# Reordering the stages of the first pass in a fused gated-attention and feed-forward kernel, moving weight rounding, state products, gates and the last sums

## Chip, cores and metric

One core of one Trainium2 chip. The metric is the device time of one execution in microseconds (us), median over runs. The kernel before takes 637.3 us (636.75 to 637.35, three runs).

Engines are named as in the profile: PE is TensorE (matrix products), PEld its weight loads, DVE is VectorE, ACT is ScalarE, POOL is GpSimd, SP is the engine that issues most transfers.

## The reference

Two parts, the first feeding the second. A gated linear attention keeps one 48x48 state for each of 8 heads and each batch; its rows become x of a feed-forward layer with 3072 tokens.

```python
f = 1.0 / (1.0 + np.exp(-f_logit))                    # the gate
for t in range(S):                                    # S = 768, B = 4, H = 8, D = 48
    state = f[:, :, t, :, None] * state + np.einsum('bhd,bhe->bhde', k[:, :, t], v[:, :, t])
    y[:, :, t] = np.einsum('bhd,bhde->bhe', q[:, :, t], state)
x = y.transpose(0, 2, 1, 3).reshape(B * S, H * D)     # 3072 x 384
h = x @ w_in                                          # 384 x 2048
sp = np.maximum(h, 0.0) + np.log1p(np.exp(-np.abs(h)))
return (h * erf(sp)) @ w_out                          # 2048 x 384
```

## The kernel before

The attention runs on chunks of 128 tokens, the feed-forward layer on blocks of two chunks. Chunks are numbered from 0, so the fourth chunk is chunk 3; the recorded texts also say "the sixth chunk" where they mean chunk 6, the first chunk of the fourth block. Each chunk passes four stages: `stage_d` (decays: a product of the gate's logarithms with a triangle, two exps on ScalarE, two multiplies on VectorE), `stage_t` (eight transposes, copied to `qT` and `kT`), `stage_s` (scores, their masking `A` on VectorE, then the state product `dS` and the sums `Sn` and `Mbd`) and `stage_y` (the chunk's output, copied to `xT`).

```python
def prepare(blk, j0, j1):                             # the gate of a block: log(1 + exp(-f))
    nc.vector.tensor_scalar(out=lt, in0=lt, scalar1=LOGIT_MIN, scalar2=None, op0=ALU.max)
    use_exp_ln()                                      # loads a function table, where another one is in
    nc.scalar.activation(out=lt, in_=lt, func=AF.Exp, scale=-1.0)
    nc.scalar.activation(out=lt, in_=lt, func=AF.Ln, bias=1.0)

def stage_s(g):
    sc = ...                                          # scores: 8 products
    A = ...; nc.vector.tensor_tensor(out=A, in0=sc, in1=tri, op=ALU.mult)
    if c == NCH - 1: return
    dS = ps_at.tile(..., tag="at")                    # a PSUM buffer that the next transposes need
    ...                                               # state products, 8
    for r in range(2):
        nc.vector.tensor_tensor(out=Sn[rows(r)], in0=dS[rows(r)], in1=old[...], op=ALU.add)
        nc.vector.tensor_tensor(out=new[...], in0=Sn[rows(r)], in1=total, op=ALU.mult)   # Mbd
    # total is Tall: the chunk's last row of decays, brought to other partitions by a transfer
# [cut]
```

Between the stages TensorE runs the feed-forward products. One such product is a "slot", and a schedule says at which slot which stage, which gate and which step of weight rounding (six on VectorE for each piece of 128x768, one on ScalarE) is issued:

```python
for it in range(n_blocks):
    gen, n = slots(it)
    if it == 0:
        todo = [(stage_d, 3), (stage_t, 3), (stage_d, 4), (stage_s, 3), (stage_t, 4), (stage_y, 3),
                (stage_d, 5), (stage_s, 4), (stage_t, 5), (stage_y, 4)] + stages(2)[4:]
        at = [3, 9, 12, 15, 20, 23, 36, 44, 60, 74, 78, 82, 86, 92]
    # [cut: later passes spread their stages evenly]
    if it + 3 < n_blocks:
        prepare_at = at[todo.index((stage_d, (it + 3) * CPB))] - 10     # the gate, 10 slots ahead
    for s, _ in enumerate(gen):
        due += 1 if it == 0 and s < 48 else 0.5       # rounding steps due at this slot
        # [cut: rounding, loads, stages that are due]
        if it == 0 and s == 5:
            prepare(2, 0, CPB)                        # the third block's gate
        if it + 3 < n_blocks and s == prepare_at:
            prepare(it + 3, 0, CPB)
```

The output product `project` ends with three sums on VectorE (`plus`) and the store. The kernel is scheduled by hand: the order in which this code issues instructions is the order in which each engine is given them, and that order is nearly all that the change alters.

## Time and profile before

| | before |
|---|---|
| median, range (3 runs) | 637.3 us, 636.75 to 637.35 |
| span of the profiled run | 635.8 us |
| TensorE busy | 610.8 us (96%) |
| VectorE, ScalarE busy | 428.5 us (67%), 354.2 us (56%) |
| mean granted clock | 0.992 |

TensorE is near its limit over the whole, so only its idle 25 us and the stretches of low clock can be had. The prediction below shows the lines by stretch and by wait. Two more places of the kernel before matter for what came out. The first is the gate that chunk 6 waits for in pass 0. These are timeline lines (start, duration, engine, line, operation, output<-input, in brackets the engine's idle time before it and what ended it), first ScalarE, then VectorE, then TensorE:

```profile
83.53 1.28 ACT L322 ACT_TABLE_LOAD   x1
89.43 0.84 ACT L339 ACTIVATE lt<-lt 128x768 f32<-128x768 f32 x1 [4.62 <-DVE lt L335]
...
88.84 0.55 DVE L335 TENSOR_SCALAR lt<-lt 128x768 f32<-128x768 f32 x1
...
91.20 0.91 PE L358 MATMUL ps_d<-lt,tri 128*128 128x384 f32 x2 [1.47 <-ACT lt L340]
```

The reader is to see that the gate's first step (L335) reaches VectorE only at 88.84, behind a queue of rounding and of the activation's multiply; ScalarE stands idle 4.62 us for it, and TensorE 1.47 us. The second place is in the steady passes, in the view of waits of TensorE's weight loads (us in total, times, longest):

```profile
PEld hps L513 <- DVE scratch L649: 1.0, 3, 0.4
```

Three waits of up to 0.4 us: nothing in a busy table, yet each is time of the bound engine.

### The profile page before, as it was taken

How to read it: one execution, taken by the hardware profiler on the slowest of the kernel's cores; microseconds unless marked ns; L12 is line 12 of the kernel's file. 1: busy time of each engine (PE TensorE's matmuls, PEld its weight loads, DVE VectorE, ACT ScalarE, POOL GpSimd, SP SyncE). 2: the span in 40 equal slices, each digit the busy share in tenths (PEclk: the TensorE clock that was granted, in tenths of full speed). 3: DMA queues.
4: the chain of work that ended last, by engine and by line, in shares of the span. 5: the costliest groups of instructions: out<-in, count | busy, mean ns of one | idle time of the engine just before them, and what ended most of it. 6: DMA issues, size and time to landing. Idle time of an engine off the chain costs nothing.

```text
span 635.8 us, 11231 instructions
## 1 busy us (share of the span) xinstructions
PE 610.8 (96%) x4727; PEld 536.7 (84%) x4727; DVE 428.5 (67%) x651; ACT 354.2 (56%) x421; POOL 25.7 (4%) x24
## 2 busy tenths in 40 slices
PE   8979899999998999999999999999999999999995
PEld 6857778788667889889889989988978989989995
DVE  4799999635899576586485584495585764756741
ACT  5354456657763675756664856666566446656200
POOL 0000000000392000000000000000000000000000
PEclk9999999999999999999999999999999999999998
DMA  9998802311211131031041041031000000000000
GB/s 198 244 278 230 258 13 51 73 26 28 51 31 32 28 75 26 14 88 26 14 89 25 14 89 25 13 76 32 19 26 1 2 26 1 10 17 1 26 26 29
DMA packets 120633, 37.02 MB, mean 58 GB/s; under 512 B 112384, under 2 KB 115456, under 8 KB 120576
## 3 DMA queue, kind: packets, MB, share of 16 engines
q1 hardware_dynamic: 118496, 35.84, 24.2%
q8 instruction: 39, 0.64, 0.4%
q10 hardware_dynamic: 2080, 0.39, 0.4%
q14 instruction: 18, 0.15, 0.1%
HBM read 31.46 MB, written 4.72 MB: 57 GB/s over the span
## 4 chain that ended last, share of the span: by engine, by line
PE 72%; DVE 15%; ACT 7%; issue 3%; DMA 2%; SPq 0%; POOL 0%; DVEq 0%; ACTq 0%; POOLq 0%
PE hps L513 30%; PE ops L641 28%; PE y L146 5%; PE sc L403 3%; PE ps_t L385 2%; PE ps_d L358 2%; ACT x L155 2%; DVE e L160 1%; DVE A L417 1%; DVE scratch L541 1%; DMA Hg<-in_moe_w_in_dram 1%; DVE w_in_sb L296 1%; DVE Hg L305 1%; PE dS L431 1%; DVE Hg L487 1%
## 5 line engine op out<-in xcount | busy, mean ns | idle before, releaser
L513 PE MATMUL hps<-xT,w_in_sb 128*128 128x256 f32 x1152 | 263.9, 384 | 1.0 <-ACT xT L460 0.6
L513 PEld LDWEIGHTS hps<-xT,w_in_sb 128*128 128x128 f32 x1152 | 216.5, 191 | 35.7 <-issue 2.6
L160 DVE SCALAR_TENSOR_TENSOR e<-x,e 128x1024 f32<-128x1024 f32 x96 | 120.0, 1250 | 23.6 <-ACT x L155 23.5
L155 ACT ACTIVATE x<-Hg,serf_bias 128x1024 f32<-128x1024 f32 x88 | 97.7, 1142 | 0.1
L641 PE MATMUL ops<-wT,Hg 128*128 128x192 f32 x352 | 86.8, 328 | 0.0
L152 ACT ACTIVATE e<-Hg 128x1024 f32<-128x1024 f32 x44 | 46.5, 1058 | 70.9 <-DVE Hg L487 70.4
L641 PE MATMUL ops<-wT,scratch 128*128 128x192 f32 x320 | 75.1, 326 | 0.8 <-DVE scratch L541 0.8
L641 PE MATMUL ops<-w_out_sb,Hg 128*128 128x192 f32 x352 | 74.3, 328 | 0.0
L487 DVE TENSOR_TENSOR Hg<-Hg,e 128x1024 f32<-128x1024 f32 x44 | 54.2, 1231 | 28.7 <-ACT e L485 28.6
L520 ACT COPY Hg<-hps 128x1024 f32<-128x1024 f32 x44 | 44.4, 1009 | 50.2 <-PE hps L513 49.8
L649 DVE TENSOR_TENSOR scratch<-scratch,ops 128x384 f32<-128x384 f32 (+1 forms) x44 | 21.1, 501 | 65.3 <-ACT scratch L657 56.2
L641 PEld LDWEIGHTS ops<-wT,Hg 128*128 128x128 f32 x352 | 61.7, 190 | 2.2 <-issue 0.2
L641 PEld LDWEIGHTS ops<-w_out_sb,Hg 128*128 128x128 f32 x352 | 60.0, 190 | 3.7 <-issue 1.2
L641 PEld LDWEIGHTS ops<-wT,scratch 128*128 128x128 f32 x320 | 55.8, 190 | 1.1 <-POOL wT L541 1.1
L485 ACT ACTIVATE e<-e 128x1024 f32<-128x1024 f32 x48 | 50.5, 1052 | 6.2 <-DVE e L160 6.2
L371 DVE TENSOR_TENSOR qd<-qn,dp 128x384 f32<-128x384 f32 x24 | 13.3, 556 | 52.9 <-ACT dp L361 52.9
L417 DVE TENSOR_TENSOR A<-sc,tri 128x1024 f32<-128x1024 f32 x24 | 29.3, 1219 | 14.8 <-PE sc L403 14.6
L641 PE MATMUL ops<-w_out_sb,scratch 128*128 128x192 f32 x160 | 39.1, 326 | 0.0
L460 ACT COPY xT<-y 128x384 f32<-128x384 f32 x24 | 11.5, 479 | 45.7 <-PE y L146 45.7
L146 PE MATMUL y<-A,vt 128*32 128x128 f32 x768 | 35.2, 277 | 1.3 <-ACT qT L391 1.2
L146 PEld LDWEIGHTS y<-A,vt 128*32 128x32 f32 x768 | 27.3, 109 | 8.2 <-issue 3.8
L403 PEld LDWEIGHTS sc<-qT,kT 48*128 48x128 f32 x384 | 24.1, 193 | 7.6 <-issue 6.3
(108 smaller groups left out, 658.8 us busy)
## 6 DMA issues: line engine op xcount, KB each, us to landing
lt<-in_f_logit_dram SPq DMA_DIRECT2D x24, 192.0 KB, 3.5
qn<-in_q_dram SPq DMA_DIRECT2D x24, 192.0 KB, 3.7
out_dram<-scratch SPq DMA_DIRECT2D x12, 384.0 KB, 3.2
kn<-in_k_dram SPq DMA_DIRECT2D x23, 192.0 KB, 3.7
vt<-in_v_dram SPq DMA_DIRECT2D x23, 192.0 KB, 2.8
w_out_sb<-in_moe_w_in_dram SPq DMA_DIRECT2D x4, 768.0 KB, 6.0
Hg<-in_moe_w_in_dram SPq DMA_DIRECT2D x4, 768.0 KB, 6.7
Hg<-in_moe_w_out_dram SPq DMA_DIRECT2D x4, 768.0 KB, 6.4
```

Source lines behind the costliest of these rows:

```text
L146: nc.tensor.matmul(y[M * i : M * (i + 1), kt, :], lhsT=terms[n][0], rhs=terms[n][1], start=(n == 0), stop=(n == len(terms) - 1), skip_grou ...
L152: nc.scalar.activation(out=dst[:], in_=h, func=AF.Exp)
L155: nc.scalar.activation(out=dst[:], in_=h, func=AF.Tanh, bias=serf_bias[:, i : i + 1], scale=SERF_KAB[i][0])
L160: nc.vector.scalar_tensor_tensor(out=e[:], in0=x[:], scalar=SERF_KAB[i][2], in1=e[:], op0=ALU.add, op1=ALU.mult)
L403: nc.tensor.matmul(sc[:, r, a, :], lhsT=kT[rows(r), a, :], rhs=qT[rows(r), a, :], start=True, stop=True,)
L417: nc.vector.tensor_tensor(out=A[:].rearrange("s r a t -> s (r a) t"), in0=sc[:].rearrange("s r a t -> s (r a) t"), in1=tri[:].unsqueeze(1) ...
L485: nc.scalar.activation(out=e[:], in_=e[:], func=AF.Tanh, scale=SERF_C)
L487: nc.vector.tensor_tensor(out=h, in0=h, in1=e[:], op=ALU.mult)
L513: nc.tensor.matmul(hps[:, j, :], lhsT=w_in_sb[:, kt, ft * P : (ft + 1) * P], rhs=xTs[blk][:, kt, :], start=(kt == 0), stop=(kt == n_k - 1),)
L520: nc.scalar.copy(out=gr["h"], in_=hps[:])
L641: nc.tensor.matmul(place[n], lhsT=x[:, j, :], rhs=y, start=(gi == 0 and j == 0 and n in first), stop=(gi == n_g - 1 and j == 1), skip_grou ...
L649: nc.vector.tensor_tensor(out=out, in0=x, in1=y, op=ALU.add)
```

## The change

Its intent is to take away TensorE's waits in the early passes: the fourth chunk (chunk 3) goes through all its stages before the fifth begins (less sharing of `qT`, `kT` and PSUM), the state product stands ahead of the scores so that its PSUM buffer is read sooner, w_out is rounded a little later, and at the end the last products have a PSUM tile of their own so that two of the three last sums can go earlier. The gates move too: that of the third block from slot 5 to 17, all later ones from 10 to 14 slots ahead of their stage.

```diff
-    xpool = main.enter_context(tc.tile_pool(name="xpool", bufs=3))
+    xpool = main.enter_context(tc.tile_pool(name="xpool", bufs=2))
@@ stage_s
+        if c < NCH - 1:
+            state(g, c)                     # dS, Sn, Mbd: now ahead of the scores and of A
         sc = ps_sc.tile([P, 2, HP, P], FP32, name="sc", tag="sc")
         # [cut: scores, A]
-        if c == NCH - 1:
-            return
-        dS = ps_at.tile([P, HP, D], FP32, name="dS", tag="at")
@@ project: two sums earlier in the last block only (end), the products in another order in all blocks
+        ops.append(ps_sc.tile([P, 2, 512], FP32, name="ops", tag="sc") if end else ops[1])
-        yield from products((2, 3), (5, 7, 3, 4))
-        plus(o[:, 5:7, :], o[:, 4:5, :].broadcast_to((P, 2, DH)), pair(5))
+        yield from products((2, 3), (5, 7))
+        if end:
+            fives()                         # the first of the three sums
+            plus(o[:, 3, :], o[:, 5, :], place[7])
+        yield from products((2, 3), (3, 4))
@@ schedule
-                todo = [(stage_d, 3), (stage_t, 3), (stage_d, 4), (stage_s, 3), (stage_t, 4), (stage_y, 3),
+                todo = [(stage_d, 3), (stage_t, 3), (stage_s, 3), (stage_y, 3), (stage_d, 4), (stage_t, 4),
                         (stage_d, 5), (stage_s, 4), (stage_t, 5), (stage_y, 4)] + stages(2)[4:]
-                at = [3, 9, 12, 15, 20, 23, 36, 44, 60, 74, 78, 82, 86, 92]
+                at = [3, 10, 15, 22, 28, 36, 42, 47, 56, 74, 77, 82, 87, 93]
-                prepare_at = at[todo.index((stage_d, (it + 3) * CPB))] - 10
+                prepare_at = at[todo.index((stage_d, (it + 3) * CPB))] - 14
-                due += 1 if it == 0 and s < 48 else 0.5
+                due += (1 if s < 42 else 0.6 if s < 72 else 0.3) if it == 0 else 0.42 if it == 1 else 0.6
-                if it == 0 and s == 5:
+                if it == 0 and s == 17:
                     prepare(2, 0, CPB)
```

## The prediction

> **What bounds the kernel now.** I read the page's totals first, then the table by stretches, then TensorE's waits, then the chain of waits, and last the timelines of the places that those named. A "slot" below is one matrix product of the hidden layer (two records) or of the output (two records); attention stages are put between slots. Pass 0 is the 96 slots of the first two token blocks, pass 1 and pass 2 the next ones, and from pass 3 on output and hidden products alternate. The passes' limits come from the order of TensorE's instructions laid on its timeline: 32.15, 103.3, 135.3 and 188 us.
>
> Table by stretches (the four early passes, then two steady stretches):
>
> ```profile
> 32.15:103.30 71.15, 63.04 (x484) 51.00 (x481) 68.31 (x98) 36.88 (x50) 0.00 (x0) 0.95 0.66 179
> 103.30:135.30 32.00, 30.76 (x270) 25.48 (x270) 20.17 (x30) 18.39 (x24) 0.00 (x0) 1.00 0.31 57
> 135.30:188.00 52.70, 51.94 (x358) 38.28 (x357) 37.12 (x38) 38.81 (x43) 18.58 (x11) 1.00 0.17 31
> 188.00:208.70 20.70, 17.79 (x175) 16.27 (x173) 20.28 (x29) 8.23 (x10) 6.02 (x6) 1.00 0.17 40
> 208.70:464.00 255.30, 255.16 (x2006) 228.43 (x2002) 159.90 (x247) 162.91 (x189) 0.00 (x0) 1.00 0.20 41
> 475.00:629.00 154.00, 153.92 (x1031) 144.80 (x1029) 91.33 (x147) 69.06 (x75) 0.00 (x0) 1.00 0.03 11
> ```
>
> The columns are TensorE, its weight loads, VectorE, ScalarE, GpSimd, granted clock, DMA share and GB/s. The reader is to see two kernels: VectorE is busy 68.31 of 71.15 us in pass 0 (96%), and again from 188 to 209; outside, 409 us are TensorE alone. The change removes no matrix product, so those 409 us stay, and only the early part, one place near 470 and the last 7 us can move.
>
> TensorE's waits over the whole span, and the timelines around them:
>
> ```profile
> PE ps_t L385 <- DVE Sn L444: 5.9, 4, 2.1
> PE ps_d L358 <- ACT qT L391: 2.0, 1, 2.0
> PE ps_d L358 <- ACT lt L340: 1.5, 1, 1.5
> PE y L146 <- ACT qT L391: 1.2, 1, 1.2
> PE ps_t L385 <- DVE qd L371: 1.1, 1, 1.1
> PE ps_t L385 <- ACT qT L391: 0.7, 1, 0.7
> PE hps L513 <- ACT xT L460: 0.6, 1, 0.6
> ...
> 41.25 0.84 ACT L339 ACTIVATE lt<-lt 128x768 f32<-128x768 f32 x1 [4.74 <-DVE lt L335]
> 42.13 0.84 ACT L340 ACTIVATE lt<-lt 128x768 f32<-128x768 f32 x1
> 42.88 0.57 ACT L391 COPY qT<-ps_t 128x512 f32<-128x512 f32 x1
> ...
> 77.73 0.66 PE L385 MATMUL ps_t<-ident,kd 128*128 128x128 f32 x4 [1.99 <-DVE Sn L444]
> ...
> 43.50:48.30 4.80, 4.80 (x24) 3.52 (x24) 4.70 (x8) 3.76 (x6) 0.00 (x0) 0.64 1.11 320
> 78.00:86.00 8.00, 8.00 (x32) 6.50 (x30) 7.71 (x12) 4.08 (x5) 0.00 (x0) 0.79 0.12 25
> ```
>
> The first group is what the change aims at. The transposes wait four times until the state product's PSUM buffer is read, because VectorE multiplies the scores (1.22 us) before it reads it. The copy of qT stands in ScalarE's queue behind the gate's exp and ln, which wait for VectorE. The last two lines show a hidden cost: after each of the two 2.0 us waits the granted clock falls to 0.64 and 0.79, which costs (1-0.64)*4.8 = 1.7 and (1-0.79)*8 = 1.7 us more.
>
> The end of the span:
>
> ```profile
> 628.96 0.56 DVE scratch L649
> 629.52 0.03 issue
> 629.55 0.82 DVE scratch L649 x2
> ```
>
> Three sums in a row stand between the last product and the last store.
>
> **The Trainium skill.** "TensorE: Matmul & The Clock Gate", Part 1, says that the array's clock falls to half when it has idled for a window of about 3.4 us. The trace agrees on the effect, but shows it after waits of only 2.0 us. The same page, under "Architectural detail", calls the queues of ScalarE and VectorE strict FIFO; the qT copy behind the gate's exp and ln agrees (transposes done at 39.7, copy begun at 42.88). "ScalarE: Activation LUTs", "What ACT_TABLE_LOAD costs", gives 1283 ns a load; the trace has 1.28 us for each. "PSUM", "PSUM bank collisions", wants readers and writers of a bank kept apart; the change does that at the end with a third tile, and the trace of before has no such overlap to compare.
>
> **The change part by part.** Durations: a slot is 0.44 us (42 records in 9.26 us in the chain), ps_d 0.65, the eight transposes 0.87, scores 1.09, dS 0.49, y 1.69. VectorE's six rounding steps of a weight piece follow each other in 4.64 us.
>
> 1. Fewer x buffers (3 to 2). The next x is preceded on ScalarE by an exp that already waits for VectorE's multiply with the older e, so VectorE has by then read the old x. Cost 0.
>
> 2. Rounding later. The order of instructions on VectorE shows how little moves: ahead of the sixth chunk's A there are two steps fewer (1.5 us), and all rounding still ends in pass 1. The first eight pieces, which the hidden products need, keep their places. By itself this is worth at most 1.5 us.
>
> 3. Fourth chunk first. I walk through pass 0 with VectorE running without a gap from its first step after y of chunk 2. VectorE starts it 0.6 us earlier (the state sums no longer wait behind A), y of chunk 2 comes 0.7 us later, so pass 0 begins at 32.9.
> - Transposes of chunk 3: TensorE there at 32.9+11*0.44+0.65 = 38.4, kd at 38.2: the 1.1 us wait is gone. The qT copy no longer stands behind the gate's exp: the 2.0 us wait and its slow clock (1.7) are gone.
> - New: y of chunk 3 stands at slot 22, reached at 46.9. Its A comes on VectorE after pieces 1, 2, 3, most of 4 and the state sums, at 50.1. A wait of 3.2 us.
> - New: y's copy stands on ScalarE behind the exp and ln of the next block's gate, whose VectorE step ends at 52.4, and behind one rounding step: xT is there at 55.4, TensorE at 52.3. A wait of 3.1 us, with one slow-clock stretch, 1.7 us.
> - From 55.4 to the sixth chunk's ps_d lie 54 slots (23.8 us), two ps_d, two sets of transposes, one scores with dS, one y (6.3 us) and the slow clock 1.7: 87.2. VectorE has the state sums of chunk 4 read 0.5 us after TensorE wants the buffer: 87.7. The gate (VectorE 85.9, ScalarE 87.6) is just in time; before it cost 1.5 us.
> - Before, this ps_d ran at 91.2, and 12.1 us from there to the end of pass 0 remain in both. Gain 3.5, of which I count 3.0, as two waits so close may slow the clock twice.
>
> 4. Pass 1. Ideal is 48*0.44 plus the stages of chunks 6 and 7, 8.95: 30.1 against 32.0 before. But y of chunk 6 still waits for qT behind the gate (my walk: 1.9 us, before 1.2). One table load of 1.28 us less. Gain 0.3.
>
> 5. State ahead of scores. In pass 2 (0.76 us) the wait goes; in pass 3 the 2.09 us shrink by the 1.14 us of A that no longer lies in front; near 470 the 1.07 us go. Together 0.8+1.1+1.1 = 3.0. The fourth, 1.99 us, is in pass 0 and counted there. Three ScalarE- and VectorE-bound passages (163 to 208) begin with VectorE waiting for TensorE's ps_d, so they move with it.
>
> 6. The end. Two of three sums move under the last 16 products (5.2 us): 1.41-0.56 = 0.8 us.
>
> Sum: 3.0+0.3+3.0+0.8 = 7.1 us, and 637.3-7.1 = 630.2 us.
>
> **The rivals.**
> - VectorE is the bound of pass 0, and a new order cannot shorten 68 us of its work. For it: the 96%, and the two new waits that I found. Against it: the waits behind A and behind the gate happen where TensorE has products ready. Then pass 0 gains nothing or loses 2 us: 633 to 635.
> - The new waits are avoided because steps are shorter or fall otherwise than I walk, and the slow clock is gone too. All 8.1 us of waits and 3.4 us of slow clock in pass 0 would go: 637.3-11.5-4.1 = about 622. Against it: VectorE has no room for that.
> - The early lead is given back in 163 to 208, where VectorE is full (20.28 of 20.70 us), its sums beside GpSimd taking 1.1 us. For it: that stretch has its own chain of e, x and Hg. Against it: VectorE idled 8.6 and 5.6 us before. It would leave only parts 5 and 6, about 633.5.
>
> **Range and chances.** My largest uncertainty is pass 0, from -1 to +8. Passes 2, 3 and the end are firm to about 1.5 us. I take 626 to 635.5. Faster by 2% means below 624.6, which needs nearly all of the second rival: 0.08. Slower by 2% needs a new stall of 20 us, for which nothing speaks: 0.02. Within: 0.90.
>
> **What would show it.** Right: pass 0 ends near 100 instead of 103.3, with waits of y on A or of hps on xT near 3 us and none of ps_d on qT; the waits of transposes on Sn fall from 5.9 to under 2 us; one sum after the last product; the steady stretch as long as before. Wrong: VectorE idle in pass 0, or the lead at 100 us gone at 209 us. The prediction fails if the two new waits don't come, or if they slow the clock for longer than 1.7 us.

## The result, and the profile after

| | before | after |
|---|---|---|
| median, range (4 runs each, same chip) | 637.33 us, 636.75 to 638.06 | 629.21 us, 629.11 to 630.11 |
| ratio after to before | | 0.9875 (95%: 0.9858 to 0.9892) |
| span of the profiled run | 635.8 us | 627.4 us |
| granted clock of that run | 0.992 | 0.992 |

Ratios here and below are the mean time of one kernel's runs over that of the other's of the same rounds, so not quite the ratio of the medians. The change is 1.25% faster.

Where the time came from: the same products are looked up in both traces, and the lead is the difference of their times. The y of chunk 5, whose end is taken as the end of pass 0, stands one slot (0.44 us) later in the new schedule, which is added back.

| landmark | lead of after, us | gained since the line above | predicted |
|---|---|---|---|
| start of pass 0 | 0.41 | 0.4 | |
| end of pass 0 | 102.01 - 99.84 + 0.44 = 2.6 | 2.2 | 3.0 (with the start) |
| end of pass 1 | 129.21 - 126.86 = 2.35 | -0.2 | 0.3 |
| end of pass 2 | 176.33 - 173.03 = 3.3 | 0.95 | 0.8 |
| end of pass 3 | 208.83 - 204.26 = 4.6 | 1.3 | 1.1 |
| steady passes, to 428 | 428.02 - 421.88 = 6.1 | 1.6 | 0 |
| past the place near 470 | 478.73 - 471.17 = 7.6 | 1.4 | 1.1 |
| end of span | 635.8 - 627.4 = 8.4 | 0.85 | 0.8 |

The table by stretches of the kernel after, its limits moved by those leads (columns as in the prediction: TensorE, weight loads, VectorE, ScalarE, GpSimd, clock, DMA share, GB/s):

```profile
31.74:100.72 68.98, 61.00 (x484) 50.20 (x481) 64.23 (x93) 36.19 (x49) 0.00 (x0) 0.95 0.68 185
...
204.13:457.86 253.73, 253.73 (x2016) 229.07 (x2012) 163.15 (x251) 162.20 (x188) 0.00 (x0) 1.00 0.20 41
```

The lead of 0.41 us at the start is not the change's work as far as the runs show: the first hidden product starts between 31.1 and 32.2 us in the fourteen profiles, and in b_prep below, which changes nothing before it, 0.7 us earlier than in before.

Pass 0 is 2.2 us shorter, but TensorE is still idle in it for 68.98 - 61.00 = 8.0 us (before 8.1): the waits of before were replaced more than removed. What fell is the busy time, from 63.04 to 61.00 us for the same products. Most of that is the clock: both kernels have 6.83 us at a clock of 0.50 in pass 0, but in before TensorE is busy through all of them, in after for 3.84 us, because one of its slow stretches falls into a wait. At half speed a busy microsecond loses a half, so as an estimate the slow clock costs 3.4 us before and 1.9 us after. The steady stretch is 1.6 us shorter with the same products. The waits of TensorE's products in the kernel after:

```profile
PE y L146 <- DVE A L419: 6.0, 2, 5.0
PE ps_t L385 <- DVE Sn L446: 2.7, 2, 1.7
...
PE y L146 <- ACT qT L391: 1.7, 1, 1.7
...
PE hps L515 <- ACT xT L462: 1.1, 1, 1.1
```

The four waits on Sn (5.9 us) are now two (2.7), those of ps_d on qT and on lt are gone, and y waits for A 5.0 us at one place. That place in the timelines of VectorE and TensorE:

```profile
46.02 0.34 DVE L446 TENSOR_TENSOR Sn<-dS,Mbd 48x192 f32<-48x192 f32 x1
48.53 0.35 DVE L449 TENSOR_TENSOR Mbd<-Sn,Tall 48x192 f32<-48x192 f32 x1 [2.16 <-DMA Tall<-dp]
...
49.67 1.23 DVE L419 TENSOR_TENSOR A<-sc,tri 128x1024 f32<-128x1024 f32 x1
...
50.95 0.66 PE L146 MATMUL y<-A,vt 128*32 128x128 f32 x8 [5.02 <-DVE A L419]
```

The stretch of that wait and the one in which y runs, columns as above:

```profile
46.00:50.00 4.00, 0.00 (x0) 0.00 (x0) 1.76 (x6) 0.00 (x0) 0.00 (x0) 0.74 1.12 321
50.00:54.00 4.00, 3.05 (x56) 2.54 (x56) 3.93 (x6) 0.73 (x1) 0.00 (x0) 0.50 0.91 233
```

During the wait VectorE is busy only 1.76 of 4 us: it idles 2.16 us until the transfer of Tall has landed (issued between 41.27 and 43.92), because Mbd now stands ahead of A. From 50 us on it is full again (3.93 of 4). The clock is 0.50 from 50 to 54 us, and 0.90 for the next 4.

The end of the span holds one sum after the last product instead of three:

```profile
618.80 0.94 DVE L653 TENSOR_TENSOR scratch<-scratch,ops 128x384 f32<-128x384 f32 x2 [1.69 <-PE ops L645]
621.40 0.56 DVE L653 TENSOR_TENSOR scratch<-scratch,ops 128x384 f32<-128x384 f32 x1 [1.66 <-PE ops L645]
```

### The profile page after: what moved, and what is told of

It reads as the page before. It is cut to its first block, busy times and chain, and to the rows that moved or that the text cites. A ratio compares the mean times of both kernels' runs of the same rounds, so it can differ in the third digit from the quotient of the medians. Undisturbed runs are those within 1.5% of the kernel's fastest.

```text
span 627.4 us, 11233 instructions
## 1 busy us (share of the span) xinstructions
PE 605.7 (97%) x4727; PEld 536.8 (86%) x4727; DVE 428.1 (68%) x651; ACT 351.8 (56%) x419; POOL 25.6 (4%) x24
## 4 chain that ended last, share of the span: by engine, by line
PE 80%; DVE 9%; ACT 6%; DMA 2%; issue 1%; SPq 1%; POOL 0%; DVEq 0%; POOLq 0%; ACTq 0%
PE hps L515 34%; PE ops L645 31%; PE y L146 5%; PE sc L414 3%; PE ps_t L385 3%; PE ps_d L358 2%; ACT x L155 1%; DVE e L160 1%; DMA Tall<-dp 1%; PE dS L433 1%; DVE scratch L543 1%; DVE A L419 1%; DMA lt<-in_f_logit_dram 1%; PE busy L348 1%; ACT e L152 1%
## 5 line engine op out<-in xcount | busy, mean ns | idle before, releaser
L146 PE MATMUL y<-A,vt 128*32 128x128 f32 x768 | 36.5, 283 | 7.7 <-DVE A L419 6.0
L146 PE MATMUL y<-qT,Mbd 128*32 128x128 f32 x480 | 31.2, 280 | 0.0
```

Of the source, the lines that this page charges most:

```text
L146: nc.tensor.matmul(y[M * i : M * (i + 1), kt, :], lhsT=terms[n][0], rhs=terms[n][1], start=(n == 0), stop=(n == len(terms) - 1), skip_grou ...
```

## The experiments

The theory: the new order of pass 0 and the state ahead of the scores carry the 8.1 us, 3 us each, and the earlier gate is a detail. Its rivals: the earlier gate carries the most, because the wait on lt, the slow clock after it and the waits of the steady passes hang on it; or the parts work only together. So these parts were added alone to the kernel before, and all but the end part undone alone in the kernel after, where the rounding was undone too. (Letters of theories in the texts are explained there and hold for that text.) All kernels below gave correct results.

| run | time, us | ratio to before (95%) | in us of 638 |
|---|---|---|---|
| b_state: before + state ahead | 634.55 | 0.9944 (0.9925 to 0.9963) | -3.6 |
| b_fourth: before + new order of pass 0 | 639.95 | 1.0025 (1.0001 to 1.005) | +1.6 |
| b_prep: before + gate 14 slots ahead | 631.11 | 0.9895 (0.9876 to 0.9914) | -6.7 |
| b_tail: before + end part | 637.75 | 0.9997 (0.9979 to 1.0015) | -0.2 |
| a_prep10: after, gate 10 ahead | 635.42 | 0.9958 (0.994 to 0.9976) | -2.7 |
| a_state_off: after, scores first | 632.72 | 0.9919 (0.9901 to 0.9936) | -5.2 |
| a_fourth_off: after, old order of pass 0 | 628.13 | 0.9863 (0.9836 to 0.989) | -8.7 |
| a_round_off: after, old rounding | 630.16 | 0.9874 (0.9855 to 0.9893) | -8.0 |
| n_gate12_late3: see below | 627.64 | 0.9839 (0.9822 to 0.9856) | -10.3 |
| n_gate1: see below | 627.36 | 0.9834 (0.9817 to 0.9851) | -10.6 |
| n_gate1_slow: see below | 623.92 | 0.9784 (0.9766 to 0.9801) | -13.8 |
| a_slow: see below | 628.93 | 0.9861 (0.9843 to 0.9879) | -8.9 |
| after | 629.21 | 0.9875 (0.9858 to 0.9892) | -8.0 |

The median of before was 638.35 beside the first four, 638.09 beside the next four, 637.29 beside the three called n and 637.26 beside a_slow; so kernels of different groups are compared by their ratios.

### One part alone, added to the kernel before

**b_state** moves the state product (and, for the first three chunks, the product that makes Tall) ahead of the scores and nothing else.

```diff
+        if c < NCH - 1:
+            state(g, c)
         sc = ps_sc.tile([P, 2, HP, P], FP32, name="sc", tag="sc")
```

> The kernel before with one part of the change: totals and state products ahead of the scores, everything else as before. Theory A (my prediction's sum): the waits of the transposes on the state sums (Sn) fall from 5.9 us to about 1.7; outside pass 0 this is worth 3.0 us, and as pass 0 is bound by VectorE's work, its own wait of 2.0 us and the slow clock after it come back elsewhere: 3.0 to 3.5 us faster in all. Theory B (pass 0 is bound by waits, not by VectorE's sum): the pass-0 wait (1.1 us of the 2.0) and its slow clock of 1.7 us count too: about 6 us faster, and the granted clock near 78 to 86 us is 1.00.

**b_fourth** takes the new `todo` and `at` of pass 0, and with them the third block's gate at slot 17.

```diff
-                todo = [(stage_d, 3), (stage_t, 3), (stage_d, 4), (stage_s, 3), (stage_t, 4), (stage_y, 3),
+                todo = [(stage_d, 3), (stage_t, 3), (stage_s, 3), (stage_y, 3), (stage_d, 4), (stage_t, 4),
-                at = [3, 9, 12, 15, 20, 23, 36, 44, 60, 74, 78, 82, 86, 92]
+                at = [3, 10, 15, 22, 28, 36, 42, 47, 56, 74, 77, 82, 87, 93]
-                if it == 0 and s == 5:
+                if it == 0 and s == 17:
```

> The kernel before with only the new order of attention stages in pass 0 and the gate of the third block at slot 17 instead of 5. Theory A: the new waits (y on A, hidden products on xT, together 5 to 6 us, and a slow clock after them) nearly pay for the old ones that go (qd 1.1, qT 2.0 and 0.7, slow clock 1.7): 0 to 2 us faster. Theory B: the new order is the main source of the gain of pass 0: 2.5 us or more faster.

**b_prep** is one number:

```diff
-                prepare_at = at[todo.index((stage_d, (it + 3) * CPB))] - 10
+                prepare_at = at[todo.index((stage_d, (it + 3) * CPB))] - 14
```

> The kernel before with only the gate prepared 14 slots ahead of its stage instead of 10. Theory A (my prediction, which counted this only in pass 0): at most 1.5 us faster, and the stretch from 210 to 464 us is as long as before. Theory B (formed on the two traces): in every steady pass ScalarE copies the first output product 0.2 to 0.5 us too late, behind the gate's table loads, exp and ln, so that the first hidden product waits for its PSUM buffer; the earlier gate ends that. Then the distance between the 42-record runs of hidden products of consecutive passes falls by about 0.3 us each, some 1.9 us over the six passes, and the whole is 2 to 3.5 us faster.

**b_tail** takes the end of `project` alone, with its third PSUM tile:

```diff
+        ops.append(ps_sc.tile([P, 2, 512], FP32, name="ops", tag="sc") if end else ops[1])
-        yield from products((2, 3), (5, 7, 3, 4))
+        yield from products((2, 3), (5, 7))
+        if end: ...                                   # two of the three sums
+        yield from products((2, 3), (3, 4))
```

> The kernel before with only the last block's products 3 and 4 in the scores' PSUM and two of the three last sums moved ahead (the order of products 5, 7, 3, 4 changes in all blocks too). Theory A: one sum of 0.56 us after the last product instead of 1.41 us, 0.85 us faster, and nothing else moves. Rival: the store that follows waits for its queue anyhow, or the order of products in the other blocks costs something: 0 to 0.4 us.

Measured: the state part is worth 3.6 us by time. The new order of pass 0 costs 1.6 us, just clear of the noise (0.1 to 3.2); the waits it removed came back as one of 4.4 us of the hidden products on xT and one of 1.5 us of y on A. The gate alone gives 6.7 us, most of what the whole change gives. Both were missed: no theory had b_fourth slower, and for b_prep the two theories had at most 1.5 and 2 to 3.5 us. The end part is inside the noise by time, 0.8 us by span (635.8 to 635.0). The largest of TensorE's waits, first in b_fourth, then in b_prep:

```profile
PE hps L513 <- ACT xT L460: 4.4, 1, 4.4
```

```profile
PE ps_t L385 <- DVE Sn L444: 3.2, 2, 1.9
```

In b_prep the wait on lt is gone, and two of the four waits on Sn with it: those of pass 2 and near 470. Its lead over before, with the 0.72 us by which its start happened to be earlier taken off, is 1.7 us at the end of pass 0, 2.1 after pass 1, 3.0 after pass 2, 2.7 after pass 3, 4.3 at 428 and 5.8 at the end. So the gate reaches far past pass 0, and the 1.6 us of the steady passes, which the prediction had as zero, are its work: in a_prep10 below, where it alone is undone, the lead over before is 0.2 us at the end of pass 3 and 0.2 at 428. There the earlier gate also moves ScalarE's table load and its copy of the first output product (L657) away from the moment at which the next hidden products need that PSUM buffer; the wait of weight loads on L649, shown for before, is not in the list of b_prep.

### One part undone in the kernel after

**a_prep10** turns 14 back to 10:

```diff
-                prepare_at = at[todo.index((stage_d, (it + 3) * CPB))] - 14
+                prepare_at = at[todo.index((stage_d, (it + 3) * CPB))] - 10
```

> The changed kernel with the gate prepared 10 slots ahead again. Theory A (the parts overlap: either the earlier gate or the state sums ahead remove the waits of passes 2 and near 470): only what the earlier gate alone does comes back, the wait of the sixth chunk's ps_d in pass 0 (about 1.7 us) and the late PSUM buffers of the steady passes (about 1.6 us): 3 to 4 us slower than the changed kernel. Theory B (the parts add): it gives back all that it gave alone, 6 to 7 us.

**a_state_off** puts the state product behind A again (the diff of b_state, reversed).

> The changed kernel with the scores ahead of the state products again. Theory A (overlap): the wait of the transposes in pass 3 grows again by 1.1 us and that in pass 0 too, but y of the chunks 2 and 3 waits 1 and 3.6 us less for A, which no longer stands behind the state sums and their transfer: 0.5 us faster to 1.5 us slower than the changed kernel. Theory B (the parts add): it gives back what it gave alone, 2 to 3.6 us slower.

**a_fourth_off** restores `todo`, `at` and the third block's gate at slot 5 (the diff of b_fourth, reversed).

> The changed kernel with the old order of the stages of pass 0 and the gate of the third block at slot 5 again. Theory A (the new order costs as much as it did alone, 2.4 us of span): 1 to 2.5 us faster than the changed kernel, because the two new waits (6.1 us with a slow clock behind them) go and only the old ones (4.1 us with a slow clock) come back. Theory B (the new order pays only together with the state sums ahead and the slower rounding): 1 to 3 us slower.

**a_round_off** restores the old rate of rounding:

```diff
-                due += (1 if s < 42 else 0.6 if s < 72 else 0.3) if it == 0 else 0.42 if it == 1 else 0.6
+                due += 1 if it == 0 and s < 48 else 0.5
```

> The changed kernel with the rounding rates of before. Theory A (little moves): within 1.5 us, slower because two to three more rounding steps stand ahead of the state sums of chunk 4 and of the gate of chunk 6 (0.6 to 1 us each). Theory B (the rate is what gives VectorE room in pass 0): 2 us or more slower.

Measured: by the ratios, the gate undone costs (0.9958 - 0.9875) * 638 = 5.3 us, the state in the same way 2.8, both near the 6.7 and 3.6 that they gave alone. The theory by which the gate and the state overlap (3 to 4 us for the gate, at most 1.5 for the state) missed both; the one by which they add (6 to 7 and 2 to 3.6) had the second. The wait on lt is back, 2.4 us, the clock behind it is 0.60 for 4 us where the kernel after has 1.00, and the three waits of the weight loads are back. First that stretch (columns as above), then the weight loads' waits from 205 us on:

```profile
92.00:96.00 4.00, 4.00 (x12) 2.85 (x10) 2.75 (x6) 2.20 (x5) 0.00 (x0) 0.60 0.03 0
```

```profile
PEld hps L515 <- DVE scratch L653: 1.0, 3, 0.4
```

Undoing the new order costs nothing that can be seen: 0.9863 against 0.9875, not resolved from each other; neither of the theories (1 to 2.5 us faster, 1 to 3 us slower) is confirmed, and the noise leaves room for the first. (The new order and the third block's gate at slot 17 were always moved together, so which of the two costs was not tested.) Undoing the rounding changes nothing either. Added up, the parts alone give -3.6 + 1.6 - 6.7 - 0.2 = -8.9 us, against -8.0 of the whole. So in the sum the parts nearly add, and the gate carries the most.

By place they do not add. State, order and gate each on or off are eight kernels, and all eight have run. This is how much earlier than in before pass 0 ends in each profiled run, the start of pass 0 set equal (for the new order with its one slot added back; those of the kernel after have the later rounding as well):

| gate | neither | state ahead | new order | both |
|---|---|---|---|---|
| 10 slots ahead | 0 (before) | -2.4 (b_state) | -3.0 (b_fourth) | -2.9 (a_prep10) |
| 14 slots ahead | +1.7 (b_prep) | +4.1 (a_fourth_off) | +0.4 (a_state_off) | +2.2 (after) |

With the old gate, moving anything makes pass 0 longer: TensorE comes sooner to chunk 6 and waits there for lt, 3.4 us in b_state and 2.5 in b_fourth, where before waits 1.5. Each number is one profiled run, and that of a_fourth_off is its fastest, so the 4.1 is on the high side. The slow clock is in these numbers too: half of TensorE's busy time at 0.50, the estimate used above, is 3.4, 3.4, 4.1 and 3.0 us in the upper row and 3.4, 0, 2.7 and 1.9 in the lower. With these taken out the gate still gains in every column (1.7, 3.1, 2.0 and 4.0 us). The new order costs 0.9 to 2.3 us in three pairs and nothing between a_fourth_off and after. That the state gains in pass 0 once the gate is earlier is not shown: without the slow clock it loses 1.0 us in one pair and gains 1.0 in the other. Outside pass 0 the gate removes a wait in pass 2 and the one near 470 which the state removes as well, so there the two do not add.

a_fourth_off showed one thing more. Its four runs are 626.52, 627.79, 628.48 and 630.9 us, at granted clocks of 0.999, 0.999, 0.995 and 0.991: one program, 4.4 us apart. Its profiled run has the same wait of ps_d on qT, 2.00 us to the hundredth, as b_prep has, and what follows differs. First a_fourth_off, its line of the timeline and three stretches around it, then b_prep, its line and the stretch of the wait with the one behind it:

```profile
40.99 0.91 PE L358 MATMUL ps_d<-lt,tri 128*128 128x384 f32 x2 [2.00 <-ACT qT L391]
```

```profile
36.56:39.97 3.41, 2.28 (x13) 1.43 (x11) 3.31 (x6) 1.20 (x2) 0.00 (x0) 1.00 0.82 255
39.97:43.39 3.42, 2.40 (x19) 1.70 (x21) 3.32 (x5) 3.42 (x6) 0.00 (x0) 1.00 1.10 313
43.39:46.80 3.41, 3.41 (x40) 3.00 (x35) 3.34 (x7) 1.37 (x3) 0.00 (x0) 1.00 1.12 308
```

```profile
42.78 1.34 PE L358 MATMUL ps_d<-lt,tri 128*128 128x384 f32 x2 [2.00 <-ACT qT L391]
```

```profile
39.73:43.14 3.41, 1.14 (x4) 0.60 (x4) 3.31 (x6) 2.57 (x5) 0.00 (x0) 1.00 1.08 327
43.14:46.55 3.41, 3.41 (x8) 2.02 (x6) 3.34 (x7) 3.37 (x6) 0.00 (x0) 0.50 1.11 308
```

The clock stays 1.00 in the one and is 0.50 for 3.41 us in the other. The kept traces say what decides it. In all fourteen, the clock is either 1.00 or 0.50, each stretch at 0.50 (but for those that the end of the span cuts off) lasts 3.41 us or two or three times that, and the changes of one trace lie whole multiples of 3.41 us apart (figures between 0.50 and 1.00 in the lines of this document are means over a change). The stretches above are cut at these places. With every trace cut so, a stretch at full clock in which TensorE's products were idle for 1.91 us or more in sum is always followed by one at 0.50 (30 of them), and one with 1.84 us or less never is (2488). In b_prep the wait (40.78 to 42.78) lies in one stretch, which is idle for 3.41 - 1.14 = 2.27 us; in a_fourth_off (38.99 to 40.99) it is split over two, idle for 1.13 and 1.02 us. So the same wait costs about 1.7 us or nothing, by where it falls. Where these places lie differs from run to run (the first lies 4.8 to 7.5 us after the start of the span in the fourteen traces), which can make one program spread; the runs without a trace cannot be checked for it.

### Can the new waits be taken away?

**n_gate12_late3** is the kernel after with chunk 3's state behind its scores (the others stay ahead) and the third block's gate at slot 12.

```diff
-        if c < NCH - 1:
+        late = g in LATE and c < NCH - 1              # LATE = (3,)
+        if c < NCH - 1 and not late:
             state(g, c)
@@ behind A
+        if late:
+            state(g, c)
-                if it == 0 and s == 17:
+                if it == 0 and s == 12:
```

> After, with two things changed in pass 0 only: chunk 3's state product stands behind its scores again (all others stay ahead), and the next block's gate is issued at slot 12 instead of 17. Theory (the new order of pass 0 costs because y of chunk 3 waits 5.0 us for A, which stands on VectorE behind state sums that wait for a transfer, and because x's transpose stands behind the gate): both waits shrink below 2.5 us in sum, the clock of 46 to 58 us no longer falls to 0.5, and the time is 2 to 4 us below after, 625 to 627. Rival (VectorE is full in pass 0, so a wait taken away comes back at the next stage): the time stays within 1 us of after, 628 to 630, with new waits of ps_d on lt or of transposes on Sn of 3 us or more.

**n_gate1** is the kernel after with the old order of pass 0 and the third block's gate at slot 1.

> After, with the old order of pass 0 and the gate of the third block issued at slot 1 instead of 5. Against the run that had the old order and slot 5 (628.1, waits of ps_d on qT 2.0 and of y on qT 2.1). Theory (the copy of qT stands behind the gate's exp on ScalarE): both waits fall below 1 us each and the time is 1 to 3 us lower, 625 to 627. Rival (VectorE full): the waits turn into longer ones on Sn or A, and the time stays at 628 to 629.

**n_gate1_slow** is that with later rounding:

```diff
-                due += (1 if s < 42 else 0.6 if s < 72 else 0.3) if it == 0 else 0.42 if it == 1 else 0.6
+                due += (1 if s < 42 else 0.3) if it == 0 else 0.6
```

> The same with rounding of w_out put off further (from slot 42 of pass 0 at 0.3 steps a slot, 0.6 later). Theory (the waits of transposes on Sn, 3.1 us in three, stand behind rounding steps that need not be there yet): they fall to about 1 us, and the time is 1 to 2 us below the run without it, 623 to 625. Rival (rounding is off the path, as the run with the old rates showed): within 0.7 us of it.

**a_slow** is the kernel after with only this rounding.

> After with only the rounding of w_out put off further, as in the best run of before (0.3 steps a slot from slot 42 of pass 0 instead of 0.6, 0.6 later instead of 0.42). Theory (VectorE is full from slot 42 on, so nine steps fewer between slots 42 and 72 free TensorE's waits there in any order of the stages): the wait of transposes on Sn at 76.8 us (1.7) goes, the 5.0 us wait on A, which is earlier, stays, and the time is 1.5 to 3 us below after: 626 to 627.5. It then stays about 2 to 3 us above the old order with the same rounding (623.9), which is the cost of the new order. Rival (the slower rounding helps only the old order, whose gate wait of 2.2 us it took away): the time equals after within 0.7 us, 628.5 to 630.

n_gate12_late3 is 627.64, between the two theories, and its waits say why: y on A fell from 5.0 to 1.7 us at that place and xT is gone, but the transposes of the next chunk wait 3.2 us for qd, on a VectorE that is busy 3.86 of 4 us. The wait, then the two stretches around its start:

```profile
59.87 1.11 PE L386 MATMUL ps_t<-ident,qd 128*128 128x128 f32 x4 [3.24 <-DVE qd L372]
```

```profile
54.00:58.00 4.00, 2.63 (x13) 1.97 (x11) 3.86 (x6) 2.87 (x4) 0.00 (x0) 1.00 1.17 256
58.00:62.00 4.00, 2.13 (x9) 2.10 (x10) 3.93 (x7) 0.72 (x2) 0.00 (x0) 0.58 1.00 322
```

So part of the rival held: in this stretch the wait moves rather than goes. n_gate1, at 627.36, lies between its two theories too and is not resolved from a_fourth_off's 628.13. The wait of ps_d on qT is gone, but y now waits 1.1 us on A in pass 0, the waits of y on qT stay at 2.1 us in sum (each below 1 was expected), and ps_d waits 2.2 us on lt as it did in a_fourth_off. Then n_gate1_slow gave 3.4 us more, twice what was expected. VectorE had been the queue in front of those waits, and with nine rounding steps fewer between slots 42 and 72 the wait on lt is not in its list:

```profile
PE y L146 <- DVE A L419: 2.1, 2, 1.1
...
PE ps_t L385 <- DVE Sn L446: 1.7, 2, 0.9
...
PE y L146 <- ACT qT L391: 1.3, 1, 1.3
```

With no wait over 1.3 us from 30 us on (each line's third number is the longest), the clock is 1.00 in every stretch looked at between 46 and 106 us. At 623.92 us this is the fastest kernel, 2.2% below before (2.0 to 2.3), and it beats the kernel after as well.

a_slow missed: 628.93 against an expected 626 to 627.5. As expected the long wait on Sn went (0.9 us is left). But y waited 6.2 us for A instead of 5.0, as the transfer of Tall was late again (VectorE idle 3.32 us for it, against 2.16 us in the kernel after), and the clock behind it was lower for longer (0.50 from 54 to 58 us and 0.68 to 62, where after has 0.90 and 1.00). The wait and the stretch behind it:

```profile
51.61 0.66 PE L146 MATMUL y<-A,vt 128*32 128x128 f32 x8 [6.18 <-DVE A L419]
```

```profile
54.00:58.00 4.00, 3.12 (x21) 1.82 (x14) 3.83 (x6) 3.97 (x6) 0.00 (x0) 0.50 0.88 244
```

So the rival was right in its number, and its reason, that the slower rounding helps the old order alone, holds as far as these four kernels go. In the old order, with the third block's gate at slot 1, the same rounding is (0.9861 - 0.9784) * 638 = 4.9 us better, intervals apart: that is what the new order and its later gate cost together there. Most of it is the clock, by the estimate used above: 10.24 us at 0.50 in a_slow's pass 0, of which TensorE is busy 8.0, lose 4.0 us, and n_gate1_slow has none.

## Why the prediction was right or wrong

The time was right, 629.2 against 630.2 and well inside the range, with a sum of which some terms were exact and the one for pass 0 had the wrong cause. That the sum came so near is in part luck: pass 0 and pass 1 gave less than their terms, and 1.6 us of the steady passes, counted as zero, made up for it.

1. *Fewer x buffers, cost 0.* Not tried alone, so it stays open; the other parts add up to more than the whole without it.
2. *Rounding at most 1.5 us.* Right: undoing it gave a ratio of 0.9874 against 0.9875. The slower rate of n_gate1_slow shows that the part was too small to matter, not that rounding is off the path.
3. *"Fourth chunk first ... Gain 3.5, of which I count 3.0".* This step failed, though 2.6 us came. The new order by itself costs 1.6 us, and its undoing costs nothing. What was gained in pass 0 hangs on the gate, four slots earlier: state and order without it end pass 0 2.9 us later than before, with it 2.2 us earlier (of these 5.1 us some 1.1 are the slow clock). The walk had put the gate down as "just in time; before it cost 1.5 us", as a clause of this part. The earlier gate was never made a part of its own: its one-number diff is worth 6.7 us alone and 5.3 us when undone. The mechanism in the walk, two new waits, was right and mis-sized: y on A 5.0 us (predicted 3.2) and hidden products on xT 1.1 (predicted 3.1), 6.1 us against 6.3 in sum. A began at 49.67, close to the predicted 50.1, but for another reason: the walk had VectorE "running without a gap", where it idled 2.16 us for a transfer. The walk also let pass 0 begin at 32.9, 0.7 us later than before; y of chunk 2 did wait 1.0 us for A, but the run began earlier and pass 0 with it, at 31.74.
4. *Pass 1, gain 0.3.* It was -0.2. The wait of y on qT is 1.7 us (predicted 1.9), so the wait was right and the rest, half a microsecond, is within what the walk can do.
5. *State ahead, 0.8 + 1.1 + 1.1.* Right in size: 0.95, 1.3 and 1.4 in the three places, 3.6 us alone and 2.8 us undone. But in pass 2 and near 470 the earlier gate alone removes the same waits, so these terms belong to two parts.
6. *The end, 0.8.* Right: 0.85.

Three of the prediction's own signs of being wrong, or missing signs of being right, came as well. VectorE was idle in pass 0, 2.16 us at one place. The clock behind the new waits cost more than 1.7 us: counted in the prediction's way, (1-0.50)*4 + (1-0.90)*4 = 2.4 us from 50 to 58 us. And the waits on Sn fell to 2.7 us, not under 2.

The step that failed without being a part at all is the sentence "those 409 us stay". The steady passes gave 1.6 us. It was read from a table that shows TensorE's products busy 255.16 of 255.30 us. The Trainium skill, "Perfetto Trace Analysis", "Identifying the Most-Contended Engine", says that the busy share of products is no good measure of how close TensorE is to its limit, since pipelined instructions look smaller in the trace, and names the share of peak arithmetic and the busy share of weight loads instead. The products' share misleads, though here by looking full: the products look 99.9% busy in before and 100% in after, while the weight loads rise from 228.43/255.30 = 89.5% to 229.07/253.73 = 90.3%, and the waits lie in their list. Those shown there make 1.0 of the 1.6 us. By the ends of y the lead grows in three steps of 0.36 to 0.47 us, where these waits are gone, and in two of 0.14, whose cause was not located.

Of the rivals, the second (all waits go, about 622 us) did not happen in this change, but n_gate1_slow comes to 623.9 by the same mechanism. The first (VectorE is the bound of pass 0) is right of stretches: in n_gate12_late3 a wait came back on a VectorE that was full. The third (the lead is lost between 163 and 208 us) fell: the lead grew there. On the clock, the prediction charged 1.7 us for a long wait as if it were certain; a_fourth_off shows that it is not, and which of the 3.41 us stretches the wait falls into decides.

## What to carry to other kernels

Where an engine takes its instructions in order, ask of each long-lead chain (here the gate: VectorE, then a table load and two functions on ScalarE, then TensorE) how far ahead of its use it is issued, before reordering the stages around it: one number gave most of this change, and without it the state moved ahead lost in pass 0 what it was meant to gain. Give every line of a diff its own term in the prediction, the one-character ones too, and try the parts alone, since a sum can be right while its largest part costs time. Before the stretches of two traces are compared, compare their clocks: where a wait falls moved 1.7 us here, as much as some of the parts are worth. Before work is moved ahead of other work on an engine, look at what it waits for: a state sum that waits for a transfer holds up everything behind it.

## What the Trainium skill lacked or had wrong

- "TensorE: Matmul & The Clock Gate", section "HAM oscillation — how this bites in real kernels", gives the rule that gaps over about 3.4 us are to be avoided. Here shorter ones cost clock: a wait of 2.00 us in b_prep was followed by 3.41 us at 0.50, one of 2.4 us in a_prep10 by a mean of 0.60 over 4 us. And it is not certain: the same 2.00 us was followed by 1.00 in a_fourth_off. The page's free-running window of about 3.4 us (Part 1) fits these traces, whose clock changes only at multiples of 3.41 us. But the page has the clock halved after an idle window, where here 1.91 us of idle time in one window was enough and 1.84 us was not. One program spread by 4.4 us (626.52 to 630.9) over its runs, with clocks of 0.999 to 0.991.
- "DMA: Bandwidth & Descriptors", section "Anatomy of one DMA — SWDGE (gpsimd) path", gives a fixed cost of about 2.0 us, for transfers that GpSimd issues. The transfers of Tall here (0.5 KB, issued by SP) agree in the median, 2.1 us from issue to landing, but the longest took 6.6 us; the one that landed at 48.5 us had been issued 4.6 us or more earlier, and in the stretch before it (46 to 50 us) 321 GB/s were moved. That this traffic is the reason is not shown. The section has no figure for a small transfer beside large ones.
